# Decode block on one core: VectorE turns w_down's row sums, and all vectors take one layout (n = 8p+k)

## The chip, the cores and the metric

The kernel runs on one core of one Trainium2 chip. The metric is the device time of one execution in microseconds, the median of several runs. All runs compared below are fast-state runs.

## The reference, cut to what matters

One token passes through a block whose scales (ca, cb), shifts (sa, sb) and gates (ga, gb) are computed from a conditioning vector c: layer norm, attention over a cached sequence of 65,536 keys, a gated residual, a second layer norm, a gated GELU network, and a second gated residual. The change touches mainly the last product.

```python
# D = 1024, F = 3584, one row
h = layernorm(x) * (1 + cb) + sb
x = x + gb * ((gelu(h @ w_gate) * (h @ w_up)) @ w_down)      # w_down: [3584, 1024]
return x                                                     # [1, 1, 1024] bf16
```

## The kernel before

w_down is streamed in blocks of 512 rows. Five blocks (the "early" ones) are multiplied as rows: a 32-column stationary operand holds the activation, 512 columns of w_down move past it, and four partial sums of each result row end up on PSUM partitions 0, 32, 64 and 96. The last two blocks (the "late" ones) are multiplied as columns: 128 columns of w_down are the stationary operand, one activation column moves. This gives results in column form directly, with little work after the last bytes arrive. The partial rows must be turned into columns and added to the same PSUM tile.

```python
def col_matvec(bank, jobs, rhs, nblk, first):
    for (jb, view, k0, nk) in jobs:
        PE.wait(jb.tok)                          # the load of this piece
        for kk in range(nk):
            for j in range(nblk):                # packed columns: n = 128 j + p
                ins = pe.matmul(bank[:, j:j + 1], view[:, kk, j * P:(j + 1) * P],
                                rhs[:, k0 + kk:k0 + kk + 1], start=first, stop=True, ...)
    ...
# the end of the kernel
v = row_matvec(place_d, early, o_pad, (v_uc,), (NQ - 1, NROW * UE - NQ))
v_rows = both(row_a, 2, P)            # VectorE and ScalarE copy one PSUM bank each to row_a
late = j_d[len(early):]
col_matvec(acc_dn, late[:1], o_pad[:, :, 0], KD, True)          # 32 products
PE.wait(*v_rows)
for j, a in enumerate(plain):         # sum over partitions and turn: fp32, 128-column stationary
    pe.matmul(acc_dn[:, j:j + 1], row_a[:, a], ones1[:, :], start=False, stop=True, ...)
v = col_matvec(acc_dn, late[1:], o_pad[:, :, 0], KD, False)     # 32 products
v = ... tensor_tensor(t_dn, acc_dn, gb_nat[:, :], ALU.mult)
v = ... tensor_tensor(y_col, t_dn, x1_nat[:, :], ALU.add)
v = PE.done(pe.transpose(yT, y_col, ident[:, :]))               # [128, 8] -> [8, 128]
v = DVE.done(dve.tensor_copy(y_row, yT))
sp.dma_start(out[0, 0].rearrange("(j p) -> j p", p=P), y_row)   # 8 runs of 256 B
```

The 1024 values of a vector lie on 128 partitions; p is the partition, and j or k is the place on it. The late products give n = 128j + p ("natural" layout). The layer norm and the stationary pads use n = 8p + k. So x, gate ga, gate gb and the attention result are all held in both layouts. The natural copies are made in the middle of the kernel by TensorE transposes and small VectorE operations (cut here).

## Time and profile before

| | before |
|---|---|
| time, median of the first 3 runs | 439.82 us (438.96 to 439.94) |
| profiled span | 438.6 us |
| loaded from HBM | 185.60 MB, 423 GB/s over the span |
| last packet of the loads ends | 433.42 us |
| TensorE's last product ends | 436.29 us |
| store issued, semaphore seen | 437.30, 438.53 us |

In the profile's lines PE is TensorE's products, PEld its loads of the stationary operand, DVE is VectorE, ACT ScalarE, POOL GpSimd and SPq the queue of SyncE; L396 is line 396 of that kernel. The granted clock is the share of TensorE's full clock that the trace records as granted.

The page of the kernel before. In its DMA line each digit is the busy share of one of 40 slices, in tenths.

```profile
span 438.6 us, 8499 instructions
...
DMA  8999999999999999999999999999999999999994
...
HBM read 185.60 MB, written 0.00 MB: 423 GB/s over the span
```

The DMA engines are at least 90% busy in every slice but the first and the last, so I took work in the middle of the kernel to be hidden behind loads and the tail, the last microseconds, to be what the change can shorten. These windows of one microsecond show where the tail starts to depend on compute (columns: length, PE, PEld, DVE, ACT and POOL busy, granted clock of TensorE, DMA share, GB/s):

```profile
430.00:431.00 1.00, 0.00 (x0) 0.00 (x0) 0.37 (x1) 0.28 (x1) 0.00 (x0) 0.50 0.97 389
431.00:432.00 1.00, 0.99 (x33) 0.99 (x33) 0.00 (x0) 0.00 (x0) 0.00 (x0) 0.50 0.78 307
432.00:433.00 1.00, 1.00 (x7) 1.00 (x6) 0.00 (x0) 0.00 (x0) 0.00 (x0) 0.50 0.53 188
433.00:434.00 1.00, 1.00 (x6) 1.00 (x7) 0.00 (x0) 0.00 (x0) 0.00 (x0) 0.50 0.02 6
434.00:435.00 1.00, 1.00 (x6) 1.00 (x6) 0.00 (x0) 0.00 (x0) 0.00 (x0) 0.50 0.00 0
```

After 433 almost no load traffic is left (6 GB/s in that window, none later), while TensorE is busy all the time from 431. TensorE, not DMA, ends this kernel. The timeline of the same stretch (start, duration, engine, line, operation; in brackets the idle time before it and what ended it):

```profile
429.68 0.69 DVE L815 COPY kt_sb<-kt_ps 128x512 f32<-128x512 f32 x1 [6.82 <-PE kt_ps L419]
...
431.01 1.01 PE L396 MATMUL b<-p_row,slots 128*128 128x1 bf16 x32 [1.40 <-DMA slots<-in_B_w_down_dram]
...
431.89 3.55 PE L894 MATMUL b<-ones,kt_sb 128*128 128x1 f32 x16
...
435.30 0.99 PE L396 MATMUL b<-p_row,slots 128*128 128x1 bf16 x32
436.33 0.17 DVE L898 TENSOR_TENSOR kt_sb<-b,gb_nat 128x8 f32<-128x8 f32 x1 [5.96 <-PE b L396]
436.53 0.17 DVE L900 TENSOR_TENSOR kt_sb<-kt_sb,x_nat 128x8 bf16<-128x8 f32 x1
...
436.75 0.27 PE L903 MATMUL b<-ident,kt_sb 128*8 128x128 bf16 x1 [0.46 <-DVE kt_sb L900]
437.06 0.21 DVE L905 COPY kt_sb<-b 8x128 bf16<-8x128 bf16 x1 [0.36 <-PE b L903]
437.30 0.37 SPq L907 DMA_DIRECT2D out_dram<-kt_sb  x1
```

The 8 fp32 products against ones are 16 passes and fill 3.4 us of this tail, more than the 64 column products together. The last lines show the second cost: from the end of the addition at 436.70 to the store at 437.30, a transpose and a copy.

The price of a stationary load in the two patterns can be read in this trace too, by source line. L396 loads packed columns; L373, in the first microseconds, loads every 8th column of the rows of c and x.

```profile
L396 PEld LDWEIGHTS b<-p_row,slots x64: 104/104/291, 431.0 to 436.1; 128*128 128x128 bf16 x64
```

```profile
L373 PEld LDWEIGHTS b<-ident,kt_sb x8: 138/166/170, 7.6 to 8.0; 2*128 2x128 bf16 x8
```

A duration is not yet a rate. The instruction records show packed loads starting 26.7 ns apart, and the loads with stride 8 about 60 to 62 ns apart.

### The profile page before, as it was taken

The numbers are of one execution on the slowest core, as the hardware profiler recorded it, in microseconds if no ns is written. First come the engines' busy times: TensorE is split into PE (matmuls) and PEld (weight loads), VectorE is DVE, ScalarE is ACT, GpSimd is POOL, SyncE is SP. The second block draws the span as 40 slices with busy tenths as digits, with TensorE's granted clock in tenths as the row PEclk, the third lists the DMA queues.
The fourth block names the chain that finished last, engine by engine and source line by source line (L and its number), as shares of the span: only waits on it lengthen the run. The fifth ranks groups of instructions, "written<-read, shape, count | busy, mean of one in ns | idle before, by whom it ended". The sixth has DMA issues, their size and how long they took to land.

```text
span 438.6 us, 8499 instructions
## 1 busy us (share of the span) xinstructions
PE 305.5 (70%) x3892; PEld 203.4 (46%) x3892; DVE 206.9 (47%) x309; ACT 111.8 (25%) x165; POOL 16.8 (4%) x23
## 2 busy tenths in 40 slices
PE   0436559959696878959777895968779594675376
PEld 0112236636464556646555563646556362232124
DVE  6601025637383765827465673737477373421001
ACT  1000001533332523333351443324135334000000
POOL 9500000000000000000000000000000000000000
PEclk9995669999696988979897896969689798587665
DMA  8999999999999999999999999999999999999994
GB/s 355 430 435 439 435 432 429 429 424 433 433 430 433 431 433 430 433 436 430 436 439 433 436 428 430 430 439 430 436 430 430 430 426 429 444 428 434 415 430 173
DMA packets 7936, 185.77 MB, mean 424 GB/s; under 512 B 882, under 2 KB 882, under 8 KB 1268
## 3 DMA queue, kind: packets, MB, share of 16 engines
q1 hardware_dynamic: 7904, 185.60, 98.4%
q8 instruction: 8, 0.13, 0.1%
q14 instruction: 4, 0.03, 0.0%
q10 hardware_dynamic: 20, 0.01, 0.0%
HBM read 185.60 MB, written 0.00 MB: 423 GB/s over the span
## 4 chain that ended last, share of the span: by engine, by line
DMA 56%; PE 31%; DVE 10%; issue 1%; ACT 1%; POOL 0%; POOLq 0%; SPq 0%
DMA slots<-in_A_k_cache_dram 44%; PE kt_ps L597 16%; DMA slots<-in_B_w_down_dram 8%; PE b L667 4%; DMA slots<-in_A_v_cache_dram 4%; PE sc_ps L619 4%; PE kt_ps L419 3%; DVE selt L365 3%; DVE kt_sb L705 2%; DVE s_pad L739 1%; DVE o_red L728 1%; PE b L894 1%; PE sc_ps L648 1%; PE b L635 1%; DVE o_acc L716 1%
## 5 line engine op out<-in xcount | busy, mean ns | idle before, releaser
L597 PE MATMUL kt_ps<-ident,slots 128*128 128x128 bf16 x2048 | 156.8, 238 | 48.6 <-DMA slots<-in_A_k_cache_dram 47.9
L597 PEld LDWEIGHTS kt_ps<-ident,slots 128*128 128x128 bf16 x2048 | 136.1, 108 | 74.2 <-issue 41.8
L705 DVE COPY kt_sb<-kt_ps 128x2048 bf16<-128x2048 bf16 x96 | 117.5, 1224 | 111.5 <-PE kt_ps L597 109.8
L705 ACT ACTIVATE kt_sb<-kt_ps 128x2048 bf16<-128x2048 bf16 x32 | 60.1, 1877 | 27.7 <-PE kt_ps L597 27.7
L754 ACT ACTIVATE p_sb<-sc_ps 128x512 bf16<-128x512 bf16 x32 | 19.1, 597 | 182.4 <-PE sc_ps L648 182.4
L619 PE MATMUL sc_ps<-kt_sb,q_buf 128*32 128x512 bf16 x528 | 50.9, 420 | 0.0
L667 PE MATMUL b<-slots,p_sb 128*32 128x512 bf16 x560 | 40.1, 411 | 5.3 <-DMA slots<-in_A_v_cache_dram 4.6
L419 PE MATMUL kt_ps<-slots,h_pad 128*32 128x512 bf16 x176 | 18.0, 544 | 20.9 <-DMA slots<-in_B_w_up_dram 8.6
L716 DVE SCALAR_TENSOR_TENSOR o_acc<-o_acc,s_pad,b 128x512 f32<-128x512 f32 x28 | 20.9, 747 | 12.2 <-PE b L667 11.9
L635 PE MATMUL b<-m_sp,selt 128*128 128x16 f32 x66 | 13.0, 272 | 18.2 <-DVE m_sp L744 16.5
L667 PEld LDWEIGHTS b<-slots,p_sb 128*32 128x32 bf16 x560 | 15.5, 104 | 20.2 <-issue 5.2
L739 DVE TENSOR_REDUCE s_pad<-sc_ps 128x1 f32<-128x512 f32 x32 | 21.8, 680 | 0.0
L760 ACT ACTIVATE p_row<-sc_ps,s_pad 128x512 bf16<-128x512 f32 x32 | 21.6, 677 | 0.0
L635 PEld LDWEIGHTS b<-m_sp,selt 128*128 128x128 f32 x66 | 9.8, 188 | 23.7 <-DVE m_sp L744 21.4
L419 PEld LDWEIGHTS kt_ps<-slots,h_pad 128*32 128x32 bf16 x176 | 6.1, 125 | 30.8 <-issue 9.8
L815 DVE COPY kt_sb<-kt_ps 128x512 f32<-128x512 f32 x4 | 2.8, 692 | 33.5 <-PE kt_ps L419 33.5
L619 PEld LDWEIGHTS sc_ps<-kt_sb,q_buf 128*32 128x32 bf16 x528 | 10.9, 95 | 12.3 <-issue 4.5
L419 PE MATMUL kt_ps<-slots,s_pad 128*32 128x512 bf16 x96 | 10.9, 517 | 7.4 <-DMA slots<-in_w_mod_dram 7.4
L462 POOL TENSOR_TENSOR rs<-va,halfneg 128x1 f32<-128x1 f32 x2 | 1.1, 554 | 375.8 <-DVE va L459 375.8
L817 ACT ACTIVATE kt_sb<-kt_ps 128x512 f32<-128x512 f32 (+1 forms) x4 | 2.4, 595 | 49.0 <-PE kt_ps L419 49.0
L648 PEld LDWEIGHTS sc_ps<-ident,p_row 128*128 128x128 bf16 x136 | 7.8, 98 | 15.1 <-issue 14.4
L648 PE MATMUL sc_ps<-ident,p_row 128*128 128x128 bf16 x136 | 13.7, 224 | 0.2 <-ACT p_row L760 0.2
(107 smaller groups left out, 170.9 us busy)
## 6 DMA issues: line engine op xcount, KB each, us to landing
slots<-in_A_k_cache_dram SPq DMA_DIRECT2D x16, 4096.0 KB, 23.5
slots<-in_A_v_cache_dram SPq DMA_DIRECT2D x16, 4096.0 KB, 23.6
slots<-in_w_mod_dram SPq DMA_DIRECT2D x4, 3072.0 KB, 20.4
slots<-in_A_wq_dram SPq DMA_DIRECT2D x2, 4096.0 KB, 35.5
slots<-in_A_wo_dram SPq DMA_DIRECT2D x4, 2048.0 KB, 25.3
slots<-in_B_w_gate_dram SPq DMA_DIRECT2D x2, 3584.0 KB, 30.2
slots<-in_B_w_up_dram SPq DMA_DIRECT2D x2, 3584.0 KB, 29.5
slots<-in_B_w_down_dram SPq DMA_DIRECT2D x2, 2048.0 KB, 35.1
```

Of the source, the lines that this page charges most:

```text
L365: dve.tensor_scalar(selt[:, :].rearrange("p (r h) -> p r h", h=REP), selw[:, HQ - REP:HQ].unsqueeze(1).to_broadcast([P, NR, REP]), -scale, ...
L419: ins = pe.matmul(out, pad[:, k, :], view[:, kk, c0:c0 + ROW], start=k <= last_k[0], stop=k >= last_k[1], skip_group_check=True,)
L597: ins = pe.transpose(kt_ps[:, half * 2048 + t * P:half * 2048 + (t + 1) * P], j_k[i - i % KU].view[:, i % KU * CH + b * TB + t, :], ident[ ...
L619: ins = pe.matmul(sc(j)[QD * g:QD * (g + 1), :], q_buf[:, j % SITES, QD * b:QD * (b + 1)], kt_sb[:, j % 2, n:n + w, :].rearrange("p n d -> ...
L635: ins = pe.matmul(b6[:, 0:NR], selt[:, :], m_sp[:, j % 2, :], start=True, stop=True)
L648: ins = pe.transpose(sc_bf[:, o:o + P], p_row[:, j % 2, c * P:(c + 1) * P], ident[:, :])
L667: ins = pe.matmul(b7[QD * c:QD * (c + 1), :].rearrange("p (b d) -> p b d", b=NB), p_sb[:, s, c * P + QD * g:c * P + QD * (g + 1)], v[:, NQ ...
L705: ev[i % SITES][b].done(act.activation(dst, src, ACT.Copy) if E_ is AC else dve.tensor_copy(dst, src))
L716: v = oc[j % SITES].done(dve.scalar_tensor_tensor(o_acc[:, :], o_acc[:, :], al[:, j:j + 1], b7[:, :], ALU.mult, ALU.add))
L739: v = DVE.done(dve.tensor_reduce(m_new, sc(j), AX.X, ALU.max))
L754: pc[jt % SITES].done(act.activation(p_sb[:, jt % SITES, :], sc_bf[:, o:o + ROW], ACT.Copy))
L760: v_x[j] = ex[s].done(act.activation(p_row[:, j % 2, :], sc(j), ACT.Exp, bias=mneg[:, j:j + 1], scale=scale, accum_out=zr[:, j:j + 1],))
```

## The change

The intent is to shorten the tail. Everything moves to n = 8p + k. VectorE turns the partial rows in 32x32 blocks (reading PSUM with stride 8 so that its output is sorted by k), after which four products with a 32-column selector sum the four partitions and land in column form. The natural copies of x, ga, gb and the attention result go away, and so does the final transpose, since the 8 values of a partition are 16 contiguous bytes of the output. The price is that w_down's late columns must be taken with stride 8.

```diff
-                            bank[:, j:j + 1], view[:, kk, j * P:(j + 1) * P], rhs[...],
+                            bank[:, j:j + 1], view[:, kk, j:D:nblk], rhs[...],
 ... (the natural copies of x, ga, gb, attention and x1 are removed: 8 fp32 transposes
 ...  after the attention product, 16 small ones after the modulation, one load of x)
+        dve.tensor_reduce(sel32[:, :].unsqueeze(2), identf[:, :].rearrange("p (a r) -> p r a", r=QD), AX.X, ALU.add)
 ...
-        v_rows = both(row_a, 2, P)
+        DVE.wait(v)
+        for h in range(2):
+            v_rows = DVE.done(dve.transpose(
+                row_a[:, h * ROW:(h + 1) * ROW],
+                kt_fp[:, (2 + h) * ROW:(3 + h) * ROW].rearrange("p (a r k) -> p a k r", r=QD, k=KD)))
         late = j_d[len(early):]
         col_matvec(acc_dn, late[:1], o_pad[:, :, 0], KD, True)
-        PE.wait(*v_rows)
-        for j, a in enumerate(plain):
+        PE.wait(v_rows, v_sel)
+        turned = row_a.rearrange("p (a k r) -> p a k r", a=NQ, r=QD)
+        for a in range(NQ):
             pe.matmul(
-                acc_dn[:, j:j + 1], row_a[:, a], ones1[:, :], start=False, stop=True, ...)
+                acc_dn[QD * a:QD * (a + 1), :], sel32[:, :], turned[:, a, :, 0], start=False, stop=True, ...)
         v = col_matvec(acc_dn, late[1:], o_pad[:, :, 0], KD, False)
 ... (multiply by mod_sb[:, 5, :] and add x1_col, in place of gb_nat and x1_nat)
-        yT = b6[:, :].bitcast(dt.bfloat16)[0:KD, 768:768 + P]
-        v = PE.done(pe.transpose(yT, y_col, ident[:, :]))
-        v = DVE.done(dve.tensor_copy(y_row, yT))
-        sp.dma_start(out[0, 0].rearrange("(j p) -> j p", p=P), y_row).then_inc(out_sem, 16)
+        sp.dma_start(out[0, 0].rearrange("(p k) -> p k", p=P), y_col).then_inc(out_sem, 16)
```

More of the change, by code (lines that the diff above doesn't have):

```diff
@@ L124, in bass_adaLN_cond__gqa_block_cached__geglu_ffn__decode_kernel @@
     c_sem = nc.alloc_semaphore("c_sem")
-    x_sem = nc.alloc_semaphore("x_sem")
     out_sem = nc.alloc_semaphore("out_sem")
@@ L131, in bass_adaLN_cond__gqa_block_cached__geglu_ffn__decode_kernel @@
     ident = sb("ident", [P, P], dt.bfloat16)
-    x_col = sb("x_col", [P, KD])
-    x_nat = sb("x_nat", [P, KD])
+    cx_col = sb("cx_col", [P, 2, KD])
+    c_col, x_col = cx_col[:, 0, :], cx_col[:, 1, :]
     sg_col = sb("sg_col", [P, KD])
@@ L140, in bass_adaLN_cond__gqa_block_cached__geglu_ffn__decode_kernel @@
     halfneg = sb("halfneg", [P, 1])
-    c_col = sb("c_col", [P, KD])
     s_pad = sb("s_pad", [P, KD, QD], dt.bfloat16)
     h_pad = sb("h_pad", [P, KD, QD], dt.bfloat16)
-    ga_nat = sb("ga_nat", [P, KD])
-    gb_nat = sb("gb_nat", [P, KD])
-    att_nat = sb("att_nat", [P, KD])
-    x1_nat = sb("x1_nat", [P, KD])
     mod_sb = sb("mod_sb", [P, 6, KD])
@@ L163, in bass_adaLN_cond__gqa_block_cached__geglu_ffn__decode_kernel @@
     rsel = sb("rsel", [P, NR])
+    sel32 = sb("sel32", [P, QD])
     selt = sb("selt", [P, P])
@@ L179, in bass_adaLN_cond__gqa_block_cached__geglu_ffn__decode_kernel @@
     cx_row = kt_sb[0:2, 0, 0:KD, :].rearrange("p a b -> p (a b)")
-    x_row = kt_sb[0:KD, 0, KD, :]
     row_q = ktf(0)[:, 4 * ROW:6 * ROW]
@@ L188, in bass_adaLN_cond__gqa_block_cached__geglu_ffn__decode_kernel @@
     y_col = ktf(0)[:, 6 * P:7 * P].bitcast(dt.bfloat16)[:, 0:KD]
-    y_row = ktf(0)[0:KD, 7 * P:8 * P].bitcast(dt.bfloat16)[:, 0:P]
     kt_ps = nc.alloc_psum_tensor("kt_ps", [P, 4 * 1024], dt.bfloat16)
@@ L253, in emit_all @@
         act.dma_start(cx_row[1:2, :], A_x[0]).then_inc(c_sem, 16)
-        act.dma_start(x_row, A_x[0, 0].rearrange("(j p) -> j p", p=P)).then_inc(x_sem, 16)
         wmod_v = w_mod.rearrange("(p k) n -> p k n", p=P)
@@ L361, in emit_all @@
             rsel[:, :].unsqueeze(2), identf[:, :].rearrange("p (r h) -> p r h", h=REP), AX.X, ALU.add)
+        dve.tensor_reduce(
+            sel32[:, :].unsqueeze(2), identf[:, :].rearrange("p (a r) -> p r a", r=QD), AX.X, ALU.add)
         v = DVE.done(dve.tensor_reduce(
@@ L372, in emit_all @@
         for j in range(KD):
-            pe.matmul(b6[:, 2 * j:2 * j + 2], cx_row[:, j:D:KD], ident[0:2, 0:2], start=True, stop=True)
-        PE.wait((x_sem, 16))
-        v = PE.done(pe.matmul(b6[:, 2 * KD:3 * KD], x_row, ident[0:KD, 0:KD], start=True, stop=True))
+            ins = pe.matmul(b6[:, 2 * j:2 * j + 2], cx_row[:, j:D:KD], ident[0:2, 0:2], start=True, stop=True)
+        v = PE.done(ins)
         DVE.wait(v)
-        cx = b6[:, 0:2 * KD].rearrange("p (k c) -> p c k", c=2)
-        v_c = DVE.done(dve.tensor_copy(c_col[:, :], cx[:, 0, :]))
+        v_c = DVE.done(dve.tensor_copy(cx_col[:, :, :], b6[:, 0:2 * KD].rearrange("p (k c) -> p c k", c=2)))
         AC.wait(v_c)
-        v_th = AC.done(act.activation(th_col[:, :], c_col[:, :], ACT.Tanh, scale=0.5))
-        dve.tensor_copy(x_col[:, :], cx[:, 1, :])
-        v_x = DVE.done(dve.tensor_copy(x_nat[:, :], b6[:, 2 * KD:3 * KD]))
+        v_th = AC.done(act.activation(th_col[:, :], c_col, ACT.Tanh, scale=0.5))
         DVE.wait(v_th)
@@ L385, in emit_all @@
         DVE.wait(v)
-        v_s = DVE.done(dve.tensor_tensor(s_pad[:, :, 0], c_col[:, :], sg_col[:, :], ALU.mult))
+        v_s = DVE.done(dve.tensor_tensor(s_pad[:, :, 0], c_col, sg_col[:, :], ALU.mult))
         def col_matvec(bank, jobs, rhs, nblk, first):
@@ L396, in col_matvec @@
                         ins = pe.matmul(
-                            bank[:, j:j + 1], view[:, kk, j * P:(j + 1) * P], rhs[:, k0 + kk:k0 + kk + 1],
+                            bank[:, j:j + 1], view[:, kk, j:D:nblk], rhs[:, k0 + kk:k0 + kk + 1],
                             start=first, stop=True, skip_group_check=True,
@@ L487, in quads @@
             return t.rearrange("p (n g y) -> p n g y", n=n, g=w // QD)[:, :, :, 0]
-        hn1, v_hn1 = ln_norm(x_col[:, :], v_x, 32)
+        hn1, v_hn1 = ln_norm(x_col, v_c, 32)
         def place_m(k):
@@ L510, in emit_all @@
         v_h = modulate(h_pad, hn1, v_mod, 0, 1)
-        nat_ps = kt_fp[:, 2 * ROW:4 * ROW]
         def rest_of_mod():
@@ L516, in rest_of_mod @@
             v_tb = turn(b7[:, :], 2 * QD, high, mixed, 2 * QD, (v_rb,))
-            for i, (src, q) in enumerate(((row_m[:, 0:2 * ROW], 2), (row_m[:, 2 * ROW:4 * ROW], 1))):
-                for j, a in enumerate(plain):
-                    o = i * ROW + j * QD
-                    ins = pe.transpose(
-                        nat_ps[:, o:o + QD], src[QD * q:QD * (q + 1), a],
-                        identf[QD * q:QD * (q + 1), QD * q:QD * (q + 1)])
-            v_tn = PE.done(ins)
-            DVE.wait(v_tb)
-            dve.tensor_copy(mod_sb[:, NQ:NQ + 2, :].rearrange("p g k -> p k g"), quads(b7[:, :], KD, 2 * QD))
-            DVE.wait(v_tn)
-            nv = nat_ps.rearrange("p (i j y) -> p i j y", i=2, y=QD)[:, :, 0:KD, 0]
-            dve.tensor_copy(ga_nat[:, :], nv[:, 0, :])
-            DVE.done(dve.tensor_copy(gb_nat[:, :], nv[:, 1, :]))
+            DVE.wait(v_tb)
+            DVE.done(dve.tensor_copy(
+                mod_sb[:, NQ:NQ + 2, :].rearrange("p g k -> p k g"), quads(b7[:, :], KD, 2 * QD)))
         def place_2(b0, n):
@@ L830, in emit_all @@
         DVE.wait(v)
-        v_x1 = DVE.done(dve.tensor_tensor(x1_col[:, :], t_att[:, :], x_col[:, :], ALU.add))
+        v_x1 = DVE.done(dve.tensor_tensor(x1_col[:, :], t_att[:, :], x_col, ALU.add))
         hn2, v = ln_norm(x1_col[:, :], v_x1, 34)
-        v_tn = turn(tr_ps, P, row_a, plain, P, (v_ac,))
         v_h2 = modulate(h_pad, hn2, v, 3, 4)
-        DVE.wait(v_tn)
-        v = DVE.done(dve.tensor_reduce(att_nat[:, :].unsqueeze(2), quads(tr_ps, KD), AX.X, ALU.add))
-        DVE.wait(v)
-        v_tf = v
-        v = DVE.done(dve.tensor_tensor(att_nat[:, :], att_nat[:, :], ga_nat[:, :], ALU.mult))
-        DVE.wait(v)
-        v_xn = DVE.done(dve.tensor_tensor(x1_nat[:, :], att_nat[:, :], x_nat[:, :], ALU.add))
         NBF = F // ROW
@@ L860, in emit_all @@
         v_rows = both(row_g, 2, QD * (NBF - NQ))
-        v_g = turn_f(row_g, v_rows + (v_tf,))
+        v_g = turn_f(row_g, v_rows + (v_ac,))
         DVE.wait(v_g)
@@ L888, in emit_all @@
         v = row_matvec(place_d, early, o_pad, (v_uc,), (NQ - 1, NROW * UE - NQ))
-        v_rows = both(row_a, 2, P)
+        DVE.wait(v)
[3 more added lines that the diff above has]
+                kt_fp[:, (2 + h) * ROW:(3 + h) * ROW].rearrange("p (a r k) -> p a k r", r=QD, k=KD)))
         late = j_d[len(early):]
         col_matvec(acc_dn, late[:1], o_pad[:, :, 0], KD, True)
-        PE.wait(*v_rows)
-        for j, a in enumerate(plain):
+        PE.wait(v_rows, v_sel)
+        turned = row_a.rearrange("p (a k r) -> p a k r", a=NQ, r=QD)
+        for a in range(NQ):
             pe.matmul(
-                acc_dn[:, j:j + 1], row_a[:, a], ones1[:, :], start=False, stop=True, skip_group_check=True)
+                acc_dn[QD * a:QD * (a + 1), :], sel32[:, :], turned[:, a, :, 0],
+                start=False, stop=True, skip_group_check=True)
         v = col_matvec(acc_dn, late[1:], o_pad[:, :, 0], KD, False)
-        DVE.wait(v, v_xn)
-        v = DVE.done(dve.tensor_tensor(t_dn, acc_dn, gb_nat[:, :], ALU.mult))
         DVE.wait(v)
-        v = DVE.done(dve.tensor_tensor(y_col, t_dn, x1_nat[:, :], ALU.add))
-        PE.wait(v)
-        yT = b6[:, :].bitcast(dt.bfloat16)[0:KD, 768:768 + P]
-        v = PE.done(pe.transpose(yT, y_col, ident[:, :]))
+        v = DVE.done(dve.tensor_tensor(t_dn, acc_dn, mod_sb[:, 5, :], ALU.mult))
         DVE.wait(v)
-        v = DVE.done(dve.tensor_copy(y_row, yT))
+        v = DVE.done(dve.tensor_tensor(y_col, t_dn, x1_col[:, :], ALU.add))
         SP.wait(v)
-        sp.dma_start(out[0, 0].rearrange("(j p) -> j p", p=P), y_row).then_inc(out_sem, 16)
+        sp.dma_start(out[0, 0].rearrange("(p k) -> p k", p=P), y_col).then_inc(out_sem, 16)
         sp.wait_ge(out_sem, 16)
```

## The prediction

> **What bounds the kernel.** The loads. The DMA page shows 185.6 MB at a mean of 424 GB/s, and in the 40 slices the DMA share is 9 tenths or more in all but the first and last. The span is 438.6 us and the runs' median 439.82. The windows by single microseconds show DMA traffic dying at about 433, so only the last 7 us or so (the tail) can change the time. The granted clock there is 0.50.
>
> **The tail now** (timeline, all in us from the start): early row sums end 429.6; VectorE and ScalarE copy them, 0.69; TensorE starts the late column products at 431.01 on the landing of a w_down load and stays busy without a gap until 436.29: 32 column products (starts 26.7 ns apart, 0.86), 16 fp32 passes of the row sums against ones (213 ns apart, 3.41), 32 more column products (about 0.9). Then multiply and add on VectorE (0.4), TensorE transpose with copy (0.55 from the add's end to the copy's), store issued 437.30, its semaphore seen at 438.53 (1.23). By 433.5 all data is in, so TensorE, not DMA, ends the chain, and every microsecond after 431 is critical.
>
> **What the change removes.** (a) 16 fp32 passes with a 128-column stationary, 3.41 us. (b) Final transpose, copy and hand-overs, 0.57. (c) In the middle: 8 fp32 transposes at 391.9 (1.07 us) beside the norm chain that waits for GpSimd, three small VectorE operations after h_pad, the transposes of ga and gb, the third load of x. All off the path: loads are queued tens of us ahead there. Worth 0.
>
> **What it adds.**
> - Two 128x512 fp32 VectorE transposes out of PSUM. A copy of that shape takes 0.69; estimated 1.2 to 1.5 for both in a row, 429.7 to about 431.1. They hide behind the first 32 column products: worth 0.
> - 8 fp32 passes with a 32-column stationary. 128 columns take 213 ns, so estimated 53 to 60 ns each, with the switch between types 0.6 us in place of 3.4.
> - Stride 8 in the 64 late stationary loads. The Trainium skill, "TensorE: Matmul & The Clock Gate", Weight-path perf modes, allows fast weight load for packed or strided columns, without a price for the stride. This trace has one: the opening loads of c and x use the same stride-8 bf16 pattern and start 61 ns apart at most (138 to 170 ns each), against 26.7 apart (104 ns) for packed columns. So 32 products take about 2.0 us in place of 0.86, twice: +2.2.
> - The store in 128 runs of 16 B in place of 8 of 256 B. The skill, "DMA: Bandwidth & Descriptors" (table at its head), says that transfers below 512 B cost a read-modify-write; both are below. Eight packets per engine rather than one: estimated +0.2.
>
> **Sum.** -2.8 (sums) + 2.2 (stride) - 0.57 (transpose) + 0.2 (store) = about -1.0. Most of the gain on the sums is eaten by the strided loads. Predicted 438.8 us, range 437.3 to 440.0. Chances: faster by over 2% 0.01, within 2% 0.98, slower by over 2% 0.01.
>
> **What will show it.** Late column products' starts 60 ns apart (27 would mean the stride is free); sel32 passes about 60 ns apart; VectorE transposes done before the first 32 products end (about 433.0); TensorE's last product near 435.7; store issue near 436.1, 1.4 us to its semaphore; DMA share before 430 unchanged.
>
> **What would make it wrong.** A free stride: 2 us more gain, then the last loads end the chain (437). A 4-byte transpose at a quarter rate: it ends after 433 and the sums wait, loss of 1 to 2. 16-byte writes much slower than 0.2. The runs of before differ by 1 us, as much as the effect.

## The result, and the profile after

The changed kernel takes 438.43 us (438.31 to 438.54, 6 runs), the kernel before 439.75 us (438.96 to 439.94, 6 runs). A ratio is the mean time of one kernel's fast runs over that of the other's of the same rounds, so it is not quite the ratio of these medians: 0.9972, interval 0.9959 to 0.9985. This is a gain of about 1.3 us, which the interval calls real. Of the 34 runs of before, 4 took 438.63 to 439.00 us, 0.7 to 1.4 less than the others; no trace of such a run was kept, and the cause is open. The slowest run of after (438.54) is still below the fastest of them.

The DMA line of the page after shows that the loads still fill the kernel, as before:

```profile
DMA  8999999999999999999999999999999999999995
```

The windows after, with the columns as before:

```profile
430.00:431.00 1.00, 0.20 (x3) 0.20 (x4) 0.78 (x2) 0.00 (x0) 0.00 (x0) 0.50 0.98 391
431.00:432.00 1.00, 1.00 (x20) 1.00 (x20) 0.00 (x0) 0.00 (x0) 0.00 (x0) 0.50 0.78 301
432.00:433.00 1.00, 1.00 (x23) 0.99 (x22) 0.00 (x0) 0.00 (x0) 0.00 (x0) 0.50 0.41 158
433.00:434.00 1.00, 1.00 (x24) 0.98 (x20) 0.00 (x0) 0.00 (x0) 0.00 (x0) 0.50 0.00 0
434.00:435.00 1.00, 1.00 (x19) 1.00 (x18) 0.00 (x0) 0.00 (x0) 0.00 (x0) 0.50 0.00 0
```

TensorE is still busy without a gap from 431 to 435, with a clock of 0.50. The timeline after:

```profile
429.47 1.31 DVE L860 STREAM_TRANSPOSE kt_sb<-kt_ps 128x512 f32<-128x512 f32 x2 [7.69 <-PE kt_ps L409]
...
430.80 2.09 PE L386 MATMUL b<-p_row,slots 128*128 128x1 bf16 x32 [1.40 <-DMA slots<-in_B_w_down_dram]
...
432.82 0.29 PE L868 MATMUL b<-kt_sb,sel 128*32 128x8 f32 x8
...
433.05 2.09 PE L386 MATMUL b<-p_row,slots 128*128 128x1 bf16 x32
435.17 0.17 DVE L873 TENSOR_TENSOR kt_sb<-b,mod_sb 128x8 f32<-128x8 f32 x1 [4.39 <-PE b L386]
435.37 0.17 DVE L875 TENSOR_TENSOR kt_sb<-kt_sb,x_col 128x8 bf16<-128x8 f32 x1
435.57 0.35 SPq L877 DMA_DIRECT2D out_dram<-kt_sb  x1
```

The sums shrink from 3.55 to 0.29 us of TensorE time, but each group of 32 column products grows from about 1.0 to 2.09 us. VectorE's two transposes end at 430.78, before the first column product even starts, so they cost nothing. The stationary loads of these products, by source line:

```profile
L386 PEld LDWEIGHTS b<-p_row,slots x64: 143/166/168, 430.8 to 434.9; 128*128 128x128 bf16 x64
```

That is the duration of the opening loads with stride 8 (138 to 170 ns), and not that of packed ones (104 ns). The records show starts 60 ns apart (median), at the same granted clock of 0.50 as the packed loads in before.

A balance of the profiled tails, with stretches taken from the instruction records of each trace (in us):

| stretch | before | after | difference |
|---|---|---|---|
| start of the kernel to the first late product (a load lands) | 431.01 | 430.80 | -0.21 |
| the 32 starts of the first late group | 0.85 | 1.89 | +1.04 |
| from its last start to the first start of the second group (the sums) | 3.44 | 0.35 | -3.09 |
| second group, to the end of its last product | 0.99 | 2.09 | +1.10 |
| end of the products to the store's issue | 1.01 | 0.43 | -0.58 |
| store's issue to its semaphore | 1.23 | 1.43 | +0.20 |
| sum | 438.53 | 437.00 | -1.54 (rounded terms) |

The first line is not the change's doing: in the twelve other profiles that load lets the next work begin between 430.80 and 431.08. The rest sums to -1.33 us, which is what the medians show.

### The profile page after: what moved, and what is told of

Its sections match the earlier page's. It is cut to its first block, busy times and chain, and to the rows that moved or that the text cites. A ratio compares the mean times of both kernels' runs of the same rounds, so it can differ in the third digit from the quotient of the medians.

```text
span 437.0 us, 8422 instructions
## 1 busy us (share of the span) xinstructions
PE 306.8 (70%) x3858; PEld 201.2 (46%) x3858; DVE 206.7 (47%) x303; ACT 111.3 (25%) x164; POOL 16.8 (4%) x23
## 4 chain that ended last, share of the span: by engine, by line
DMA 55%; PE 32%; DVE 10%; issue 1%; ACT 1%; POOL 0%; SPq 0%; POOLq 0%
DMA slots<-in_A_k_cache_dram 44%; PE kt_ps L575 16%; DMA slots<-in_B_w_down_dram 7%; PE b L645 5%; PE sc_ps L597 4%; DMA slots<-in_A_v_cache_dram 4%; PE kt_ps L409 4%; DVE selt L359 3%; DVE kt_sb L683 2%; DVE s_pad L717 1%; DVE o_red L706 1%; PE b L386 1%; PE sc_ps L626 1%; PE b L613 1%; DVE o_acc L694 1%
## 5 line engine op out<-in xcount | busy, mean ns | idle before, releaser
L597 PE MATMUL sc_ps<-kt_sb,q_buf 128*32 128x512 bf16 x528 | 51.9, 428 | 0.0
L645 PE MATMUL b<-slots,p_sb 128*32 128x512 bf16 x560 | 42.0, 427 | 4.6 <-DMA slots<-in_A_v_cache_dram 3.9
L409 PE MATMUL kt_ps<-slots,h_pad 128*32 128x512 bf16 x176 | 19.4, 579 | 21.9 <-DMA slots<-in_A_wq_dram 9.5
L409 PE MATMUL kt_ps<-slots,p_row 128*32 128x512 bf16 x104 | 10.0, 543 | 4.4 <-DMA slots<-in_B_w_down_dram 3.6
```

What stands on the lines that cost most here:

```text
L409: ins = pe.matmul(out, pad[:, k, :], view[:, kk, c0:c0 + ROW], start=k <= last_k[0], stop=k >= last_k[1], skip_group_check=True,)
L597: ins = pe.matmul(sc(j)[QD * g:QD * (g + 1), :], q_buf[:, j % SITES, QD * b:QD * (b + 1)], kt_sb[:, j % 2, n:n + w, :].rearrange("p n d -> ...
L645: ins = pe.matmul(b7[QD * c:QD * (c + 1), :].rearrange("p (b d) -> p b d", b=NB), p_sb[:, s, c * P + QD * g:c * P + QD * (g + 1)], v[:, NQ ...
```

## The experiments

My theory (A) was that the stride alone makes the late products slow and gives back 2.1 us of the 3.1 that the sums save. Rival B: the pace comes from something else in the new tail, such as traffic, clock or the VectorE work beside it. Rival C: the loads end the tail anyway, and the stride is free.

### e1_after_packed: after, with packed columns (result wrong)

```diff
-  view[:, kk, j:D:nblk]
+  view[:, kk, j * P:(j + 1) * P]
```

> Kernel after with one edit: the 64 late stationary loads of w_down take packed columns (result wrong on purpose). Theory A, the stride alone doubles the pace of these products (60 ns in after, 26.7 in before): they start 27 ns apart again, the first 32 take 0.86 instead of 2.0 us, TensorE then waits for the last loads (data in at about 433), and the last product comes near 433.5 instead of 435.1: time about 436.7. Rival B, the pace of 60 ns comes from something else in the tail of after (traffic, clock, the VectorE transposes beside it): spacing stays 60 ns and time 438.4. Rival C, the loads already end the tail of after, so the stride is free: spacing 27 ns, time still 438.4.

Measured: 437.07 us (436.99 to 437.19, 5 runs), 1.36 below after (another round). The spacing is 27 ns again, at the same granted clock of 0.50:

```profile
L386 PEld LDWEIGHTS b<-p_row,slots x64: 102/104/119, 430.9 to 433.6; 128*128 128x128 bf16 x64
```

In its timeline the second group no longer runs through:

```profile
431.82 0.29 PE L868 MATMUL b<-kt_sb,sel 128*32 128x8 f32 x8
...
432.17 1.01 PE L386 MATMUL b<-p_row,slots 128*128 128x1 bf16 x24
433.40 0.29 PEld L386 LDWEIGHTS b<-p_row,slots 128*128 128x128 bf16 x8 [0.30 <-DMA slots<-in_B_w_down_dram]
433.40 0.38 PE L386 MATMUL b<-p_row,slots 128*128 128x1 bf16 x8 [0.22 <-DMA slots<-in_B_w_down_dram]
433.81 0.17 DVE L873 TENSOR_TENSOR kt_sb<-b,mod_sb 128x8 f32<-128x8 f32 x1 [2.97 <-PE b L386]
```

B falls: nothing but the pattern was changed. C falls in its strong form, since time was gained. Yet it is partly right: TensorE waits for the last load at 433.40, so only 1.36 of the 2.14 us that the stride adds to TensorE's work (1.04 + 1.10 above) comes back. My expectation of 436.7 was 0.4 too low, since I had the last data ready for TensorE near 433.1 and it was 433.4.

### e2_before_stride8: before, with stride 8 (result wrong)

```diff
-  view[:, kk, j * P:(j + 1) * P]
+  view[:, kk, j:D:nblk]
```

> Kernel before with one edit: the same 64 loads take every 8th column (result wrong on purpose). A: spacing 60 ns, and since TensorE is never idle after 431 in before, both blocks lengthen the chain by about 32 x 33 ns = 1.07 us each: time 439.75 + 2.1 = 441.9. B: spacing 27 ns, 439.75.

Measured: 441.93 us (441.83 to 442.06, 5 runs) beside 439.79 for before: +2.14, ratio 1.0047 (1.0034 to 1.0061). Here nothing of the new tail is present, and the load durations are again those of stride 8:

```profile
L396 PEld LDWEIGHTS b<-p_row,slots x64: 142/168/309, 431.1 to 438.2; 128*128 128x128 bf16 x64
```

So the price is 2.14 us in both kernels whose TensorE is never idle in the tail. A is confirmed from both sides.

### e3_turn_packed and e9_turn_packed_again: the sums alone, in the natural layout (result correct)

VectorE's turn does not need n = 8p + k. Reading the row in another order gives it for n = 128j + p, with unit stride:

```diff
 (against before; sel32 is added as in after)
-        v_rows = both(row_a, 2, P)
+        for h in range(2):
+            v_rows = DVE.done(dve.transpose(row_a[:, h * ROW:(h + 1) * ROW],
+                kt_fp[:, (2 + h) * ROW:(3 + h) * ROW].rearrange("p (j a r) -> p a j r", a=NQ, r=QD)))
-        for j, a in enumerate(plain):
-            pe.matmul(acc_dn[:, j:j + 1], row_a[:, a], ones1[:, :], ...)
+        turned = row_a.rearrange("p (h a j r) -> p h a j r", h=2, a=NQ, r=QD)
+        for a in range(NQ):
+            pe.matmul(acc_dn[QD * a:QD * (a + 1), :], sel32[:, :], turned[:, :, a, :, 0], ...)
```

> Correct result. Kernel before, natural layout, packed columns, final TensorE transpose and 256-byte runs all kept; only the row sums change: VectorE turns them with unit-stride reading (n = 128j + 32a + r) and 4 sel32 products of 8 columns replace the 8 fp32 products against ones. A: it keeps the gain of the sums (3.41 to about 0.25) without the stride; TensorE then waits for the last load near 433.1, last product near 433.5, plus the old end of the kernel (436.29 to the end, 2.26 us of span in before): time about 437.2, faster than after by about 1.2. B or C: no faster than after plus the transpose it removed, 438.4 to 439.0.

Measured: 437.64 us (437.52 to 437.79, 5 runs), ratio to before 0.9951 (0.9937 to 0.9964). The unchanged repeat on another chip was announced as

> e3 once more, unchanged, to stand beside e8 on the same chip: 437.6.

and gave 437.62 us (437.56 to 437.78), ratio 0.9949 (0.9935 to 0.9962). The sums and the end of e3's timeline:

```profile
431.87 0.29 PE L902 MATMUL b<-kt_sb,sel 128*32 128x8 f32 x8
...
433.44 0.38 PE L399 MATMUL b<-p_row,slots 128*128 128x1 bf16 x8 [0.26 <-DMA slots<-in_B_w_down_dram]
433.85 0.17 DVE L907 TENSOR_TENSOR kt_sb<-b,gb_nat 128x8 f32<-128x8 f32 x1 [2.94 <-PE b L399]
...
434.28 0.27 PE L912 MATMUL b<-ident,kt_sb 128*8 128x128 bf16 x1 [0.46 <-DVE kt_sb L909]
434.58 0.21 DVE L914 COPY kt_sb<-b 8x128 bf16<-8x128 bf16 x1 [0.36 <-PE b L912]
434.82 0.37 SPq L916 DMA_DIRECT2D out_dram<-kt_sb  x1
```

It keeps the final transpose and all natural copies, and still beats after by about 0.8 us (medians of different rounds), because the last load rather than TensorE's backlog starts its end. Keeping the layout and taking the VectorE turn is the better half of the change. It missed my 437.2 by 0.44: the last product ended at 433.82 rather than 433.5, by the same late landing as in e1, and the rest lies outside the profiled span, which is 1.49 to 1.64 us shorter than the time in e3 and 1.28 to 1.39 in before. What fills that stretch is not shown.

### e4_dve_result: e3 with VectorE turning the result as well (result correct)

```diff
-        v = PE.done(pe.transpose(yT, y_col, ident[:, :]))
-        v = DVE.done(dve.tensor_copy(y_row, yT))
-        sp.dma_start(out[0, 0].rearrange("(j p) -> j p", p=P), y_row)
+        v = DVE.done(dve.transpose(y_row, y_pad))           # 32x32 blocks
+        for a in range(NQ):
+            (sp, act)[a % 2].dma_start(o4[a], y_row[QD * a:QD * a + KD, :])   # 8 runs of 64 B each
```

> Correct result. e3 with the final TensorE transpose and copy (0.57 us) replaced by one VectorE 32x32 transpose of the result (about 0.2) and four stores of 8 runs of 64 B from two queues in place of one of 8 runs of 256 B. If four issues cost what one did (0.37 us issue, 1.23 to the semaphore): 0.35 faster than e3, about 436.9. If each further issue on a queue adds 0.3 to 0.4 us: level with e3, about 437.2.

Measured: 438.00 us (437.96 to 438.06, 5 runs), 0.36 slower than e3. The transpose took 0.21 us as hoped and the first store was issued at 434.54, earlier than in e3. The two further stores on the same two queues came after the first ones, about 0.34 and 0.41 us later, and the semaphore was complete at 436.36, against 436.05 in e3. From the last issue to the semaphore it took 1.41 us, against 1.23 in e3. So the second issue on a queue (0.41) and the longer way to the semaphore (0.18) cost more than the transpose saved (0.28). Both of my expected outcomes missed, because I had left out the second of these. The runs of 64 B in place of 256 were not tested apart from the number of issues.

### e5_store_256: after, with a store of 8 runs of 256 B (values wrong)

```diff
-        sp.dma_start(out[0, 0].rearrange("(p k) -> p k", p=P), y_col)
+        sp.dma_start(out[0, 0].rearrange("(j p) -> j p", p=P), <8 partitions of 256 B>)
```

> Kernel after with one edit: the final store takes 8 runs of 256 B from 8 partitions instead of 128 runs of 16 B (stored values wrong on purpose; it still waits for the same addition). The short runs cost 0.2 us by my theory (issue to semaphore 1.43 in after, 1.23 in before): here 1.23 again and time 438.2. Rival: the 0.2 is spread of the run, or belongs to something else: 438.4.

Measured: 438.29 us (438.17 to 438.35, 5 runs). From issue to semaphore it took 1.24 us, against 1.43 in after. The profile shows the 0.2; the times alone (0.14 apart, from different rounds) would not prove it. The queue's own waits for the store, before, after and here (us in total, times, longest):

```profile
SPq L908 <- DMA out_dram<-kt_sb: 0.8, 1, 0.8
```

```profile
SPq L878 <- DMA out_dram<-kt_sb: 1.1, 1, 1.1
```

```profile
SPq L878 <- DMA out_dram<-kt_sb: 0.9, 1, 0.9
```

### e6_before_no_middle: before, without the second layout's work in the middle (result wrong)

The transposes of ga, gb and the attention rows and the VectorE operations on them are removed. The end uses the n = 8p + k vectors in their place.

```diff
-        v_tn = turn(tr_ps, P, row_a, plain, P, (v_ac,))
-        ... tensor_reduce(att_nat ...), tensor_tensor(att_nat, ga_nat), tensor_tensor(x1_nat ...)
-        ... tensor_tensor(t_dn, acc_dn, gb_nat[:, :], ALU.mult); ... x1_nat
+        ... tensor_tensor(t_dn, acc_dn, mod_sb[:, 5, :], ALU.mult); ... x1_col
```

> Kernel before with the work of the second layout in the middle taken away (transposes of ga, gb and of the attention rows, and the VectorE operations on them; the result is wrong on purpose, since the column-layout vectors are added to natural-layout sums). My theory: off the path, 0, so 439.75 within the spread of 0.3. Rival: it frees VectorE and TensorE before the gate product and so the slots of w_down, which the chain of waits names: faster by 0.5 to 1 us, 439.0.

Measured: 439.83 us (439.74 to 439.94, 5 runs) beside 439.76 for before, ratio 1.0008 (0.9994 to 1.0021). No gain is seen, as predicted (interval -0.3 to +0.9 us). The third load of x in the opening was not taken out in this run. The chain from the copy of the attention rows to the end of h_pad lasts 5.22 us in before (388.94 to 394.16) and 5.23 us here (389.71 to 394.94).

### e7_stride2 and e7_stride4: what the stride costs by its size (results wrong on purpose, one look each)

```diff
-  view[:, kk, j:D:nblk]
+  view[:, kk, j // s * s * P + j % s : j // s * s * P + s * P : s]      # s = 2, s = 4
```

> Kernel after with stride 2 instead of 8 in the late stationary loads (result wrong on purpose). If the price comes with any unpacked pattern: 60 ns between products as with 8. If it grows with the distance (bytes fetched): between 27 and 60, near 27 to 35.

> The same with stride 4. Any unpacked pattern: 60 ns. Growing with distance: between the figure of stride 2 and 60.

Measured by source line, first stride 2, then stride 4:

```profile
L386 PEld LDWEIGHTS b<-p_row,slots x64: 102/104/118, 431.0 to 433.7; 128*128 128x128 bf16 x64
```

```profile
L386 PEld LDWEIGHTS b<-p_row,slots x64: 111/118/130, 431.0 to 433.8; 128*128 128x128 bf16 x64
```

The median spacing is 27 ns at stride 2, 33 ns at stride 4 and 60 ns at stride 8 (elements of 2 bytes, clock 0.50). So it is not the mere fact of a stride. In these runs the pattern is free at 4 bytes from one element to the next, cheap at 8 and expensive at 16. Why it is so was not tested.

### e8_stride4_layout: a layout of stride 4, stored straight (result correct)

The idea that followed: n = 512h + 4p + k needs stride 4 only, and no final transpose, if the result is stored in 256 runs of 8 B.

```diff
 (against e3)
-  view[:, kk, j * P:(j + 1) * P]
+  view[:, kk, out_cols[j]]          # slice(512 h + k, 512 (h + 1), 4)
 ... (the load of x, the copies in the second layout and the order of VectorE's turn follow the new layout)
-  (final transpose and copy)
-        sp.dma_start(out[0, 0].rearrange("(j p) -> j p", p=P), y_row)
+        sp.dma_start(out[0, 0].rearrange("(h p k) -> p h k", h=2, p=P), y_col.rearrange("p (h k) -> p h k", h=2))
```

> Correct result. e3 with the second layout changed from n = 128j + p to n = 512h + 4p + k: stride 4 in the late stationary loads (33 ns spacing in the stride-4 run, against 27 for 1 and 2 and 60 for 8), VectorE turn as in after, no final transpose, result stored straight in 256 runs of 8 B. Last product near 433.95 as in the stride-4 run; the store has 16 packets for each DMA engine where after has 8: if the price goes with the count (8 more cost 0.2 us), issue to semaphore about 1.65 and time about 437.45, 0.2 faster than e3. If 8-byte runs cost more than that each: level with e3 or slower.

Measured: 438.72 us (438.56 to 439.04, 5 runs), a clear miss. The products behaved as expected (118 ns per load, the addition's end at 434.21), and the store was issued at 434.24, earlier than in every kernel above but e1, where it was 434.21. Then it took 3.39 us. The queue's own waits show it:

```profile
SPq L918 <- DMA out_dram<-kt_sb: 3.0, 1, 3.0
```

The packets themselves had all gone by 435.40, 1.16 us after the issue; the semaphore came 2.2 us later. In after this last gap is 0.4 us. The semaphore's sixteen updates are spread from 435.71 to 437.61 here, while those of after all come within 0.18 us. The price lies in the completion, and my extrapolation from the count of packets (+0.2) did not see it.

### e10_after_more_rows: after, with one block more as rows (result correct)

```diff
-        early = [a for a in j_d if a[2] < NROW * UE]
+        early = [a for a in j_d if a[2] < (NROW + 1) * UE]
```

> Correct result. Kernel after with the sixth block of w_down moved from the strided column products to the row products (8 products of 512 columns, 1.05 us, and 32 strided products fewer, 2.0 us); the VectorE transposes then start only near 431.9 and end near 433.2. Theory A: 16 strided products wait for the sums, then 16 more follow: last product near 434.75 and time about 438.1, 0.3 faster than after. If the later transposes hold up the sums for longer than that: 438.4 or slower.

Measured: 438.04 us (437.84 to 438.09, 5 runs), as expected. Half of the strided products are replaced by row products, and VectorE's turn is now what the sums wait for:

```profile
431.92 1.31 DVE L860 STREAM_TRANSPOSE kt_sb<-kt_ps 128x512 f32<-128x512 f32 x2 [9.19 <-PE kt_ps L409]
...
433.29 0.20 PEld L868 LDWEIGHTS b<-kt_sb,sel 128*32 128x32 f32 x8 [0.17 <-DVE kt_sb L860]
```

It is another sign that the strided products are on the path, but e3 is the better cure.

### e11_half_runs: half of each 16-byte run (result wrong)

```diff
-        sp.dma_start(out[0, 0].rearrange("(p k) -> p k", p=P), y_col)
+        sp.dma_start(out[0, 0].rearrange("(p k) -> p k", p=P)[:, 0:4], y_col[:, 0:4])
```

> Kernel after with the store cut to the first 8 bytes of each 16-byte run: 128 runs of 8 B, the other half of the result not stored (wrong on purpose). In e8, 256 runs of 8 B took 3.39 us from issue to semaphore, although their last packet had left 1.15 us after the issue. If the length of the run makes the receipt late: about 3.4 us here too and time 440.4. If the number of runs or two neighbouring runs written side by side does it: about 1.4 and 438.4.

Measured: 438.49 us (438.40 to 438.71, 4 runs); issue to semaphore 1.43 us, as in after. A length of 8 bytes alone is therefore not what made e8's store slow. That leaves the number of runs (256 against 128), or 8-byte runs written side by side. These two were not separated and stay open. This run also stands in for after beside e9: on the same chip it was 0.87 us slower than e9's 437.62.

## Why the prediction was right

The predicted time was 438.8 us, within 437.3 to 440.0; measured were 438.43. That range holds the time of before as well (439.75), so the total alone proves little, and the terms have to be compared. Term by term:

- **What bounds the kernel** (the loads, with the last 7 us open to change) was right. Removing the work of the second layout in the middle gave no gain (e6).
- **Sums** (predicted -2.8) gave -3.09. This is the term that was mis-sized. The step "8 fp32 passes ... estimated 53 to 60 ns each, with the switch between types 0.6 us" scaled the 213 ns of a 128-column pass by its columns. The eight passes instead start in two fours, 6 to 7 ns apart within a four and 52 ns from one four to the next, and the whole detour took 0.35 us. The four products write to different groups of 32 output partitions. The Trainium skill, "TensorE: Matmul & The Clock Gate", Part 3 (Packing small matmuls), says that small matmuls placed on different 32x32 tiles of the array run concurrently, and gives about 4 ns per tile. I had not used it; the fours in this trace agree with it in kind. That the groups are the reason is not shown, since no run put the same products on one group. The nearest comparison, 8 fp32 passes of before with a 32-column stationary operand and one output group (L791), has starts 222 to 226 ns apart, but moves 135 columns and not 8.
- **Stride 8** (predicted +2.2) gave +2.14, by the balance and by e2. The estimate came from eight instructions in the opening of the same trace, which used the same pattern on 2 rows. That it would hold for 128 rows was assumed, and it did (60 ns). e1 shows that in the changed kernel undoing it returns only 1.36 us, since the last load then ends the chain.
- **Final transpose** (predicted -0.57) gave -0.58.
- **Store** (predicted +0.2) gave +0.20. This was partly luck: no trace had priced short runs, and the same reasoning by packet count failed in e8 (1.65 us expected, 3.39 measured). The Trainium skill's page "DMA: Bandwidth & Descriptors" (Specifications) puts transfers below 512 B at a read-modify-write; both stores are below, so that line does not tell them apart, and no run here shows the mechanism. What the runs show is 1.23 to 1.24 us for 8 runs of 256 B and 1.43 us for 128 runs of 16 B.
- **VectorE transposes** (predicted 1.2 to 1.5 us, hidden) took 1.31 us and were hidden.

In the profiles 0.21 us more of the difference lies before the tail (first line of the balance). No term had foreseen it, and the medians do not show it.

The prediction did not ask whether the two halves of the change needed each other. They don't: e3 takes the turn without the layout and is 0.8 us faster than the change.

## What to carry to other kernels

When loads fill a kernel, price a change by the few microseconds after the last loads land, and check for each saving what ends the chain next: here 2.14 us of strided loads were worth only 1.36. A new layout that removes a transpose may put its stride into the busiest operand; look in the trace for the same access pattern elsewhere and read its spacing, not just its duration. Split a change into its halves before you take it whole: the useful half may need nothing of the other.

## What the Trainium skill lacked or had wrong

- "TensorE: Matmul & The Clock Gate", Weight-path perf modes, allows fast weight load for packed or strided columns without a price for the stride. In these runs 128-column bf16 loads started 26.7 ns apart when packed, 27 at stride 2, 33 at stride 4 and 60 at stride 8 (granted clock 0.50). The skill is not silent on strides elsewhere: "SBUF — State Buffer", Specifications (TRN2), says that an access that crosses to a new 16-byte line pays a penalty and that at least two hits per line are needed for full bandwidth. It gives no time for a weight load. The runs agree in kind, since stride 8 is one element per 16 bytes, but stride 4, with two, still costs 33 against 27.
- "DMA: Bandwidth & Descriptors" has no measured time for storing a small result in many short runs. The same 2 KB took 1.23 us from issue to semaphore in 8 runs of 256 B, 1.43 in 128 runs of 16 B, and 3.39 in 256 runs of 8 B. In the last case 2.2 us of it came after the last packet, while 128 separate runs of 8 B took 1.43.
- "VectorE: DVE Perf Modes", The three transpose paths, gives a time for bf16 128x128 only; no page has one for fp32 128x512 from PSUM. Two fp32 transposes of 128x512 from PSUM took 1.31 us together, the same with a reading stride of 8 elements (after) and of 1 (e3).
